# A higher cost in the list scheduler for the sums of a triple over the columns of a bank

## Chip, cores and metric

The kernel runs on one core of one Trainium2 chip. The metric is the device time of one execution in microseconds (us); lower is better. All times below are in us unless they are marked ns.

## What is computed

A gated linear attention (heads of 48 channels, 4 batches, 8 heads, 768 positions) is followed by a bilinear feed-forward block on its output (3072 tokens, model width 384, inner width 1536). Everything is float32.

```python
f = 1.0 / (1.0 + np.exp(-f_logit))
for t in range(S):
    state = f[:, :, t, :, None] * state + np.einsum('bhd,bhe->bhde', k[:, :, t], v[:, :, t])
    y[:, :, t] = np.einsum('bhd,bhde->bhe', q[:, :, t], state)
x = y.transpose(0, 2, 1, 3).reshape(B * S, H * D)
out = ((x @ w_a) * (x @ w_b)) @ w_out
```

## The kernel before

**Blocks and units.** The tokens are worked in 8 blocks of 384 (half a sequence of one batch). The attention of one block is done in two units of four heads each. A unit has a *front* and a *core*. The front (`front_parts`) is on ScalarE two sigmoids (L326 writes `inv`, L323 writes f), on GpSimd one affine step (L329), and on VectorE two running products of f (L333, 384 columns each), a small comparison (L336), a reciprocal (L341), six running products of `inv` (L346, 128 columns each), and the products k·inv and q·F (L350, into `k_in` and `q_in`). The core is on TensorE scores (L403), transposes of k (L428), gains of the state (L452), and the two parts of the output, `within` (L501) and `across` (L527), with VectorE's mask (L416, tile `at`), ScalarE's copy of the turned k (L437, tile `kT`), VectorE's states (L479, L481, L490), ScalarE's copies of the output (L546) and SyncE's transfers into `xT` (L566). Unit s's scores follow `within` of the unit before it in one step (`within_and_scores`), so L501 and L403 stand together.

**Feed-forward.** Blocks 0 and 1 multiply with both weights plainly (`up`, L610). From block 2 on, `up_triples` (L732) uses a scheme of 15 products of half blocks in place of 18, four times for each block (j = 0 to 3). Each of the 15 beats puts 2 matmuls of 192 columns (four records in the trace) into one PSUM bank of four (`ps_f`). A bank is then emptied, either by ScalarE's copy (L1319) or by VectorE's sum of the bank's 2x192 columns onto a partial result, `add` inside `up_triples` (L724, tiles `sums` or `groups`). There are five such sums in each round j (r2, r3, u4, t2, u5), 120 in all. Larger L724 instructions sum or multiply 768 or 1152 columns of copied parts in SBUF. `down` (L834) multiplies with the output weights and has small sums of its own (L863, L866, L869). Combinations of the inputs are formed in `combine_x` (L716 on VectorE, L645 on ScalarE).

**What sets the order.** Every engine works its queue in the order in which the program emits instructions, and a planner in `by_quotients` chooses this order while the program is built. The list `main` holds the feed-forward steps in a fixed order; each is a tuple made by `on_pe` or `on`: the engine, a cost in ns, a due beat, and the function to call. Beside it stand six lines of optional steps (`for_out`, `for_x`, `core`, `fore`, `loads`, `for_ba`), each in order within itself. Ahead of each main step, `fill` takes as many optional steps as fit: a TensorE step when its inputs are planned to be ready, another engine's step when it can start within one beat (653 ns) and when `delays` finds that it would not push a main step of that engine past its due beat. The planner keeps its own clock: `now` for TensorE and `free_at` for each other engine, moved on by each step's cost. A cost therefore changes no instruction; it changes which optional steps the planner finds room for at which place.

```python
def delays(engine, start, load):
    with_it, without, copied = start + load, free_at[engine], max(free_at[ACT], last_copy)
...
        with_it, without = (max(x, ready) + cost for x in (with_it, without))
        if with_it + MARGIN > max(starts.get(due, 1 << 30), without + MARGIN):
            return True
```

Of the kernel before, what the change touches and what calls it, by code (L numbers as in the profile page):

```python
# [153 lines left out]
def by_quotients(ctx, tc, q, k, f_logit, v, moe_w_a, moe_w_b, moe_w_out, out, ident, weights, bad, ps_f):  # L154
# [149 lines left out]
    PE, DVE, ACT, POOL, SP = range(5)  # L304
# [273 lines left out]
    def products(blk):  # L578

        first = (NTG, 0)[blk] if blk < 2 else blk % 2  # L580
        return groups[:, first:first + NTG].rearrange("p g (k t) -> p g k t", k=NFT)
# [7 lines left out]
    def on_pe(load, do, *args):  # L589
        beats[0] += 1  # L590
        return PE, load, 0, do, *args

    def on(engine, load, due, do, *args, copied=False):
        return engine + COPIED * copied, load, beats[0] + due if due else 1 << 30, do, *args
# [131 lines left out]
    def up_triples(blk):  # L726

        to, tail = products(blk), None

        def emit(ps, name, j, start):  # L730
            for g in range(2):
                nc.tensor.matmul(  # L732
                    ps[:, g],
                    lhsT=sums_of_w[name][:, g, 128 * j:128 * j + 128],
                    rhs=sums_of_x[blk][name],
                    start=start and g == 0,
                    stop=True,
                    skip_group_check=True,
                )

        def times(ps, name, j, start=False):
            return on_pe(BEAT, emit, ps, name, j, start)

        def copy(due, x, ps):
            return on(ACT, 400, due, nc.scalar.copy, x, ps)

        def finish(j, c, out, v):
            yield times(v, "v6", j)
            yield copy(5, out[1, 0], v)
            a, b = (  # L750
                c[:, g].rearrange("p k i t -> p k (i t)").rearrange("p k (g t) -> p g k t", g=NTG) for g in range(2)
            )
            yield on(DVE, 1280, 0, add_steps, to.rearrange("p g (k j) t -> p j g k t", k=NI)[:, j], a, b, ALU.mult, copied=True)

        for j in range(NJ3):
            v, u, r, t = (ps_f[i][:, 0:BLK].rearrange("p (g t) -> p g t", g=2) for i in free)
            free[:] = [free[i] for i in ((2, 1, 3, 0) if j < NJ3 - 1 else (2, 3, 1, 0))]
            c = (sums, last[:, 0:2 * NI * BLK])[j % 2].rearrange("p (g k i t) -> p g k i t", g=2, k=NI, i=2)
            out = {(k, i): c[:, :, k, i] for k in range(NI) for i in range(2)}
            if j % 2:  # L760
                at = thirds.index(down_first[0])
                pairs = [thirds[(at + n) % 3] for n in (1, 2)]
            else:
                pairs = [last[:, PIECE * n:PIECE * n + PIECE] for n in range(2)]
            first, second = (x.rearrange("p (g n t) -> p g n t", g=2, n=2) for x in pairs)

            def add(due, k, i, ps, copied=False):
                return on(DVE, 470, due, add_steps, out[k, i], ps, out[k, i], copied=copied)

            yield times(v, "v1", j, True)  # L770
            yield copy(3, out[2, 0], v)
            if tail:
                yield from finish(*tail)
            yield times(u, "u1", j, True)
            yield copy(3, out[1, 1], u)
            yield times(r, "r2", j, True)
            yield add(6, 1, 1, r, True)
            yield times(v, "v2", j)
            yield copy(3, out[2, 1], v)
            yield times(u, "u2", j)  # L780
            yield copy(3, first[:, :, 1], u)
            yield times(t, "t1", j, True)
            yield copy(6, out[0, 0], t)
            yield times(v, "v3", j)
            yield copy(3, first[:, :, 0], v)
            yield on(DVE, 870, 0, add_steps, c[:, :, 1:3, 1], c[:, :, 1:3, 1], first, copied=True)
            yield times(u, "u3", j)
            yield copy(3, out[0, 1], u)
            yield times(r, "r3", j, True)
            yield add(6, 2, 1, r)  # L790
            yield times(v, "v4", j)
            yield copy(3, second[:, :, 1], v)
            yield times(u, "u4", j)
            yield add(3, 0, 0, u)
            yield times(t, "t2", j)
            yield add(5, 0, 1, t)
            yield times(v, "v5", j)
            yield copy(2 if j == NJ3 - 1 else 3, second[:, :, 0], v)
            yield times(u, "u5", j)
            yield add(3, 2, 0, u)  # L800
            yield on(DVE, 870, 0, add_steps, c[:, :, 0], c[:, :, 0], second, copied=True)
            tail = j, c, out, v
        yield from finish(*tail)
# [868 lines left out]
```

## Time and profile before

| what | value |
|---|---|
| median of 3 runs | 594.78 (593.83 to 594.9) |
| the profiled execution | 595.13 |
| its span in the profile | 593.4 |
| TensorE matmul busy | 571.1 |
| VectorE busy | 412.1 |
| ScalarE busy | 256.8 |
| L724 sums of 2x192 columns from PSUM, both tile names | 60 at 552 ns and 60 at 549 ns |
| L732, the triples' matmuls of 192 columns | 1440 records, 326 to 331 ns each |
| L834, the output's matmuls of 192 columns | 1008 records, 326 to 329 ns each |

A row of the profile gives an instruction's place in the code (L724 is line 724), its engine, what it writes and reads by the program's tile names, how often it ran, and its mean duration. PE is TensorE's matmuls, PEld its weight loads, DVE is VectorE, ACT is ScalarE, POOL is GpSimd, SP is SyncE. Matmuls overlap: two records of 192 columns start 163 ns apart though each lasts twice that. An arrow with an engine's name behind idle time tells which instruction ended it.

### The profile page before, as it was taken

How to read it: one execution, taken by the hardware profiler on the slowest of the kernel's cores; microseconds unless marked ns; L12 is line 12 of the kernel's file. 1: busy time of each engine (PE TensorE's matmuls, PEld its weight loads, DVE VectorE, ACT ScalarE, POOL GpSimd, SP SyncE). 2: the span in 40 equal slices, each digit the busy share in tenths (PEclk: the TensorE clock that was granted, in tenths of full speed). 3: DMA queues.
4: the chain of work that ended last, by engine and by line, in shares of the span. 5: the costliest groups of instructions: out<-in, count | busy, mean ns of one | idle time of the engine just before them, and what ended most of it. 6: DMA issues, size and time to landing. Idle time of an engine off the chain costs nothing.

```text
span 593.4 us, 13932 instructions
## 1 busy us (share of the span) xinstructions
PE 571.1 (96%) x5802; PEld 511.8 (86%) x5802; DVE 412.1 (69%) x786; ACT 256.8 (43%) x487; POOL 89.0 (15%) x72
## 2 busy tenths in 40 slices
PE   2899999999999999999999999999999999999996
PEld 1655655557999999999999999999999999999996
DVE  6999445599978678958895678847785165835751
ACT  5577848653122464235521444326431335135300
POOL 7365637454000000000000000000000000000000
PEclk9999999999999999999999999999999999999999
DMA  8696689089552440044004410041001100000001
GB/s 216 183 253 207 221 263 272 0 150 186 114 144 70 115 93 11 15 119 97 2 1 127 109 22 2 2 106 42 3 1 48 48 2 0 2 28 1 0 29 32
DMA packets 33560, 49.42 MB, mean 83 GB/s; under 512 B 3984, under 2 KB 25264, under 8 KB 33488
## 3 DMA queue, kind: packets, MB, share of 16 engines
q1 hardware_dynamic: 30000, 42.19, 25.8%
q0 software_dynamic: 3056, 5.92, 5.9%
q8 instruction: 47, 0.77, 0.6%
q10 hardware_dynamic: 432, 0.34, 0.2%
q14 instruction: 25, 0.20, 0.1%
HBM read 33.23 MB, written 4.72 MB: 64 GB/s over the span
## 4 chain that ended last, share of the span: by engine, by line
PE 84%; DVE 11%; issue 2%; ACT 1%; DMA 1%; SPq 0%; DVEq 0%; ACTq 0%
PE ps_f L732 35%; PE ps_f L834 28%; PE ps_f L610 13%; PE ps_y L501 2%; DVE inv L346 2%; PE ps_y L527 2%; PE ps_x L403 2%; PE ps_x L452 1%; DVE sums L724 1%; PE ps_x L428 1%; DVE groups L724 1%; DVE w_ba L83 1%; DVE q_in L350 1%; DVE f_in L333 1%; DVE spare L346 1%
## 5 line engine op out<-in xcount | busy, mean ns | idle before, releaser
L610 PE MATMUL ps_f<-xT,w_ba 128*128 128x384 f32 x288 | 95.6, 489 | 1.5 <-DMA xT<-y 1.4
L1319 ACT COPY sums<-ps_f 128x384 f32<-128x384 f32 x120 | 57.5, 480 | 75.8 <-PE ps_f L732 62.2
L610 PEld LDWEIGHTS ps_f<-xT,w_ba 128*128 128x128 f32 x288 | 53.9, 190 | 38.2 <-issue 2.2
L1319 ACT COPY groups<-ps_f 128x384 f32<-128x384 f32 x120 | 57.8, 482 | 64.3 <-PE ps_f L732 41.9
L732 PE MATMUL ps_f<-xT,w_ba 128*128 128x192 f32 x384 | 78.3, 326 | 0.0
L732 PEld LDWEIGHTS ps_f<-xT,w_ba 128*128 128x128 f32 x384 | 64.8, 190 | 0.1
L73 POOL TENSOR_SCALAR sums<-sums 128x768 f32<-128x768 f32 (+1 forms) x20 | 52.2, 2612 | 35.8 <-ACT sums L71 35.6
L732 PE MATMUL ps_f<-groups,w_ba 128*128 128x192 f32 x288 | 55.3, 328 | 0.0
L732 PE MATMUL ps_f<-x_sums,raw 128*128 128x192 f32 x288 | 53.8, 331 | 1.1 <-DVE groups L724 0.9
L329 POOL TENSOR_SCALAR inv<-inv 128x768 f32<-128x768 f32 x14 | 12.9, 923 | 265.9 <-ACT inv L326 265.8
L834 PE MATMUL ps_f<-w_out,sums 128*128 128x192 f32 x288 | 52.1, 329 | 0.3 <-DVE groups L632 0.3
L834 PE MATMUL ps_f<-w_out,groups 128*128 128x192 f32 x288 | 51.7, 328 | 0.0
L732 PEld LDWEIGHTS ps_f<-x_sums,raw 128*128 128x128 f32 x288 | 47.0, 190 | 4.1 <-DVE groups L724 2.1
L834 PE MATMUL ps_f<-spare,sums 128*128 128x192 f32 x288 | 49.0, 326 | 0.0
L732 PEld LDWEIGHTS ps_f<-groups,w_ba 128*128 128x128 f32 x288 | 47.9, 190 | 0.5 <-ACT groups L1319 0.2
L834 PEld LDWEIGHTS ps_f<-w_out,sums 128*128 128x128 f32 x288 | 47.1, 190 | 1.0 <-DVE groups L632 0.6
L834 PEld LDWEIGHTS ps_f<-w_out,groups 128*128 128x128 f32 x288 | 47.1, 190 | 0.7
L834 PEld LDWEIGHTS ps_f<-spare,sums 128*128 128x128 f32 x288 | 47.1, 190 | 0.1
L724 DVE TENSOR_TENSOR sums<-sums,groups 128x768 f32<-128x768 f32 x36 | 34.7, 964 | 13.4 <-ACT groups L1319 13.0
L724 DVE TENSOR_TENSOR sums<-ps_f,sums 128x384 f32<-128x384 f32 x60 | 32.9, 552 | 15.9 <-PE ps_f L732 14.0
L732 PE MATMUL ps_f<-x_sums,w_ba 128*128 128x192 f32 x192 | 39.4, 328 | 0.5 <-DVE sums L724 0.5
L732 PE MATMUL ps_f<-xT,raw 128*128 128x192 f32 x192 | 39.6, 329 | 0.0
(142 smaller groups left out, 851.0 us busy)
## 6 DMA issues: line engine op xcount, KB each, us to landing
raw<-w_ba POOLq DMA_DIRECT2D x11, 512.0 KB, 8.5
k_in<-in_k_dram SPq DMA_DIRECT2D x32, 144.0 KB, 4.4
q_in<-in_q_dram SPq DMA_DIRECT2D x32, 144.0 KB, 4.3
v_in<-in_v_dram SPq DMA_DIRECT2D x16, 288.0 KB, 5.7
raw<-in_moe_w_out_dram SPq DMA_DIRECT2D x6, 768.0 KB, 5.6
out_dram<-o SPq DMA_DIRECT2D x22, 192.0 KB, 1.9
f_in<-in_f_logit_dram SPq DMA_DIRECT2D x28, 144.0 KB, 3.1
xT<-y SPq DMA_DIRECT2D x45, 72.0 KB, 2.1
```

What stands on the lines that cost most here:

```text
L73: nc.gpsimd.tensor_scalar(h, h, HI_MIN, HI_MAX, ALU.max, ALU.min)
L83: nc.vector.tensor_tensor(dst[:, rows], hu[:, rows], bit[:, rows], ALU.add)
L329: nc.gpsimd.tensor_scalar(inv, inv, EXP_K, 1.0, ALU.mult, ALU.add)
L346: nc.vector.tensor_tensor_scan(inv[:, w], inv[:, w], none[:, 0:C], first, ALU.mult, ALU.add)
L403: nc.tensor.matmul(ps[h][SUB * p:SUB * p + SUB, o:o + SUB], lhsT=kf[r, tokens(n, c, p)], rhs=qf[r, tokens(n, c, p)], start=True, stop=True,)
L501: nc.tensor.matmul(ps[p][e:e + D, o:o + SUB], lhsT=t["v"][r, n, c, h * D:h * D + D], rhs=at[r, h, o:o + SUB], start=o == 0, stop=True, ski ...
L527: nc.tensor.matmul(ps[p][e:e + D, o:o + SUB], lhsT=st[j][r, n], rhs=qf[r, tokens(n, c, p)], start=False, stop=True, skip_group_check=True,)
L610: nc.tensor.matmul(ps[nm][:, 0:BLK], lhsT=w[:, kt, ft * 128:ft * 128 + 128], rhs=xT[blk][:, kt], start=kt == 0, stop=kt == NKT - 1,)
L724: nc.vector.tensor_tensor(to, x, y, op)
L732: nc.tensor.matmul(ps[:, g], lhsT=sums_of_w[name][:, g, 128 * j:128 * j + 128], rhs=sums_of_x[blk][name], start=start and g == 0, stop=Tru ...
L834: nc.tensor.matmul(to, lhsT=x[:, i // 2, i % 2], rhs=w[:, NI * (i % 2) + i // 2], start=start and i == 0, stop=i == HFT - 1, skip_group_ch ...
L1319: do(*args)
```

## The change

One number changes: the cost, in ns, under which the planner enters each of the 120 sums of `add` in `up_triples`.

```diff
             def add(due, k, i, ps, copied=False):
-                return on(DVE, 470, due, add_steps, out[k, i], ps, out[k, i], copied=copied)
+                return on(DVE, 550, due, add_steps, out[k, i], ps, out[k, i], copied=copied)
```

The tuple's other entries, the due beats among them, stay. The costs of the larger sums (870 and 1280), of ScalarE's copies (400) and of the optional steps stay as well.

## Prediction

> **What bounds the kernel now.** I read the page's busy table first, then the weight loads' waits after 125 us, then stretches of time, then the instructions in order of time.
>
> ```profile
> PE 571.1 (96%) x5802; PEld 511.8 (86%) x5802; DVE 412.1 (69%) x786; ACT 256.8 (43%) x487; POOL 89.0 (15%) x72
> ```
>
> TensorE is the bound. The change can give only what TensorE loses inside the planned part; matmul time itself stays. Who holds it up there:
>
> ```profile
> PEld ps_f L732 <- DVE groups L724: 2.1, 4, 1.2
> PEld ps_f L732 <- DVE sums L724: 1.4, 3, 0.8
> PEld ps_f L732 <- ACT sums L1319: 1.0, 4, 0.3
> PEld ps_f L732 <- ACT groups L1319: 0.6, 2, 0.4
> ```
>
> The columns are total us, times, longest. About 5 us lie before triples (L732), and most of it behind VectorE's sums (L724), which free a PSUM bank. By stretch (PE, PEld, DVE, ACT, POOL busy):
>
> ```profile
> 225.00:229.00 4.00, 3.54 (x22) 3.24 (x21) 3.74 (x7) 0.61 (x2) 0.00 (x0) 1.00 0.02 6
> 277.00:303.00 26.00, 25.14 (x295) 23.74 (x297) 23.31 (x39) 12.58 (x26) 0.83 (x1) 1.00 0.01 2
> 303.00:347.00 44.00, 44.00 (x571) 42.79 (x561) 28.93 (x63) 12.98 (x29) 0.94 (x2) 1.00 0.34 87
> 347.00:357.00 10.00, 9.75 (x58) 9.26 (x58) 8.85 (x17) 5.52 (x12) 0.72 (x1) 1.00 0.00 1
> ```
>
> TensorE has holes where VectorE is 9/10 busy; at 303 to 347, VectorE is idle a third of the time and TensorE has none. The two largest holes, in order of time (start, us):
>
> ```profile
> 225.39 2.11 PE L732 MATMUL ps_f<-x_sums,raw 128*128 128x192 f32 x12
> 225.53 0.53 DVE L724 TENSOR_TENSOR sums<-ps_f,sums 128x384 f32<-128x384 f32 x1
> ...
> 226.48 0.96 DVE L350 TENSOR_TENSOR k_in<-k_in,inv 128x768 f32<-128x768 f32 x1
> 227.36 0.55 DVE L724 TENSOR_TENSOR sums<-ps_f,sums 128x384 f32<-128x384 f32 x1
> ...
> 227.96 0.92 PE L732 MATMUL ps_f<-x_sums,w_ba 128*128 128x192 f32 x4 [0.46 <-DVE sums L724]
> ```
>
> ```profile
> 297.01 0.96 DVE L350 TENSOR_TENSOR k_in<-k_in,inv 128x768 f32<-128x768 f32 x1
> ...
> 299.62 1.48 DVE L724 TENSOR_TENSOR groups<-ps_f,groups 128x384 f32<-128x384 f32 x3
> ...
> 300.69 1.27 PEld L732 LDWEIGHTS ps_f<-x_sums,raw 128*128 128x128 f32 x8 [1.15 <-DVE groups L724]
> 300.69 1.57 PE L732 MATMUL ps_f<-x_sums,raw 128*128 128x192 f32 x8 [0.86 <-DVE groups L724]
> 301.02 0.95 DVE L350 TENSOR_TENSOR q_in<-q_in,f_in 128x768 f32<-128x768 f32 x1
> ```
>
> Both times a k_in product that nobody needs yet stands before a sum for which TensorE waits. In both the next beat (four matmul records, 0.65) comes late.
>
> **What the Trainium skill says.** (1) "Perfetto Trace Analysis", section DVE / Act Engine Instruction: the profiled interval ends with the write's acknowledgement, and the next instruction may start before that. The trace agrees: a sum lasts 0.55 alone, yet three in a row start 299.62, 300.09, 300.56 and the next instruction at 301.02, so 0.47 each. The old 470 was the spacing, the new 550 is the duration; on a full queue the planner now counts 0.08 too much per sum. (2) "PSUM — Partial Sum Buffer", section Engine vs sequencer instructions: VectorE's and ScalarE's queues are strictly first in, first out, so work put ahead of a sum delays it in full. That is what the two holes show.
>
> **The change part by part.** No instruction is added or removed: 120 sums (60 + 60 in the page's groups) are entered 80 ns dearer, and the planner puts optional steps elsewhere. I compared the built orders of both. Nothing differs before 225 us. GpSimd's order is the same; on SyncE one output store passes one xT copy near 466, whose block is used after 522, so it costs nothing. ScalarE's two sigmoids (L326, L323) go behind one or two copies at 232 and 284, and other copies trade places near 248 and 263; none then frees a bank later than its next beat. The count of switches between matmul kinds stays, so their 0.1 to 0.25 each cancel.
>
> For each hole I relaid VectorE's queue by hand in the new order, with spacings from neighbouring rows of the trace: sum 0.46, product or sum of 768 columns 0.87, of 1152 1.28, scan of 384 0.86, scan of 128 0.31 to 0.39 (0.50 before one that needs its result), mask 0.88. A beat is ready for VectorE 0.85 after it starts (366.00 to 366.85); a sum lets TensorE go 0.60 after its start (300.09 to 300.69), a copy 0.52 to 0.55. A restart costs another 0.10.
>
> 1. *228.* k_in goes from 226.48 to behind the sum of 231.03. Queue: sum 225.14, sum 225.14+0.45, two scans 0.89, sum at 226.48 instead of 227.36. It frees the bank at 227.08; TensorE arrives at 226.69+0.65 = 227.34. The hole of 0.62 and its restart go, and the three copies behind it (228.86 on, with two more restarts) come 0.9 earlier. The bank of the beat that was at 230.16 is then free at 229.29, just when TensorE gets there. Gain 0.85 (0.75 to 0.95). k_in and q_in now end at 232.4, against the scores' need at 233.3.
> 2. *251.* One scan and a reciprocal (0.40) go to the front; the sum L863 comes earlier; a restart of 0.10 goes.
> 3. *277.5.* Two scans fall behind the sum of 276.91, which starts at 276.24; hole 0.15 and restart gone: 0.25.
> 4. *293.* The second 768-column sum comes 0.5 earlier, because a scan of f falls behind it; three copies stop being late: 0.3. Here L501 and L403 (scores) move three beats back, so the mask waits for them till about 288.2 and VectorE is idle from 286.6. Behind it the sum for the bank wanted at 291.4 frees it at 291.0: it fits by 0.38.
> 5. *300.7.* k_in and q_in leave for 310 and later, where VectorE has room. The 768-column sum can start once its copy is done at 296.0; then 0.87+0.87+0.46+0.31 leads to the sum at 298.5, bank free at 299.1. TensorE, 0.55 earlier by steps 3 and 4, wants it at 299.2. Hole 1.02 and restart 0.10 go; about 0.2 comes back, because in the last quarter of a triple the copy of one beat and the matmul two beats on are too close anyway (the same 0.08 to 0.14 plus a restart stands at 376.5, 437.4, 507.5, 560.3). Gain 0.87. Their scores at 316.8-1.7 find q_in done 2 us before.
> 6. *356.* A scan falls behind two sums; first of them at 355.13, bank at 355.72, wanted 355.86: hole 0.28 and restart gone, 0.38. The hole of 0.40 at 347.2 stays: ScalarE's sigmoid makes it, and its order there is unchanged.
> 7. *414.7.* The same: 0.19.
> 8. *428.* New: L428 goes one beat (0.65) later, the kT copy and the copy behind it with it; that one frees its bank at 428.09, wanted 428.00: a hole of 0.09 and a restart, minus 0.19 (0 to 0.3).
>
> Sum: 0.85+0.10+0.25+0.30+0.87+0.38+0.19-0.19 = 2.75, with 0.1 each way from rounding per step; TensorE ends the chain from 303 to the end, so it arrives in full. The profiled execution took 595.13 (span 593.4 and 1.7 around it), which would become 592.4; the runs' median is 0.35 below that execution: 594.78-2.75 = 592.0.
>
> **The rivals.** *A, likeliest:* as summed, 592.0, own range 591.4 to 592.6. *B, the hole at 300.7 stays in part:* step 5 has a margin of 0.1 only. For: VectorE's queue there has nine steps in a row without slack. Against: it starts from a copy, not from older lateness. It gives back up to 0.9: 592.9. *C, the holes move on:* VectorE's work is the same, and the next sum is late instead; only 228 and 356 (with k_in off their queue or ample room behind) help, and the copies at 428 and 293 take 0.4: 594.78-0.85-0.38+0.4 = 593.95. Against it: VectorE idles a third of 303 to 347. *D, slower:* the mask wait of step 4. A strictly ordered queue stands idle 1.6 behind scores that were put later, with two sums, two scans and the sum that three copies wait for behind it; the same at 422 to 424 (1.2). It decides once the sum behind the mask is more than 0.38 later than laid out; then both idle times show as TensorE holes and steps 2 to 5 and 7 are lost: +1.6+1.2+0.2-0.85-0.38 = 1.8, 596.6. Against: the mask followed its scores by 0.95 to 1.15 in every case before. That nothing happens at all is excluded, as the built order differs.
>
> **How the numbers follow.** A 0.60, B 0.22, C 0.10, D 0.08. Two tenths of a per cent (1.2 us) is about what a measurement of this kernel can tell from no change. A and B are faster, 0.82; C is within, 0.10; D is slower, 0.08. A and B hold 0.82, so the range runs from the floor (all that these holes and restarts hold is some 4 us, less the 0.4 of the sigmoid: 591.2, and 0.2 for rounding: 591.0) to the top of B with its rounding: 593.6.
>
> **What would show it.** Step 1: no TensorE wait near 228, a k_in product after the sum at 231. Steps 3 to 5: TensorE busy 26 of 26 in 277 to 303, but for 0.2 at its end; VectorE idle about 1.6 ahead of the mask. Step 6: no wait near 355, one of 0.3 near 345 still there. Step 8: a short wait on a copy near 426. I am wrong if the TensorE wait for L724 after 225 stays above 1.5 us in total, or if L403 waits for q_in.

## The result, and the profile after

| | before | after |
|---|---|---|
| median, run beside each other on one chip | 595.25 (592.52 to 599.22, 17 runs) | 592.67 (590.37 to 594.15, 17 runs) |
| ratio after / before, 95% interval | | 0.9949 (0.9936 to 0.9962) |
| the profiled execution | 595.13 | 593.61 |
| its span | 593.4 | 591.8 |

The changed kernel is faster by 2.6 us by the medians, and by 2.3 to 3.8 by the ratio's interval. 592.67 lies 0.67 above the predicted 592.0 and inside the range; 0.47 of the 0.67 is the starting point, since the kernel before has 595.25 here and had 594.78 in the three runs from which the prediction counted.

The same views, in the same order, of the changed kernel. First the busy table:

```profile
PE 571.0 (96%) x5802; PEld 512.0 (87%) x5802; DVE 412.3 (70%) x786; ACT 257.5 (44%) x487; POOL 89.0 (15%) x72
```

Work is the same on every engine to within 0.7 us; 1.6 us of span are gone, so they were idle time. Then the waits of the weight loads after 125 us (total, times, longest):

```profile
PEld ps_f L732 <- ACT sums L1319: 1.2, 5, 0.3
PEld ps_f L732 <- DVE sums L724: 0.8, 3, 0.3
PEld ps_f L732 <- ACT groups L1319: 0.6, 2, 0.4
```

The wait for `DVE groups L724` (2.1) is gone, and the one for `DVE sums L724` has gone from 1.4 to 0.8: VectorE's sums hold TensorE 0.8 in place of 3.5. Waits for ScalarE went up by 0.2. By stretch (PE, PEld, DVE, ACT, POOL busy):

```profile
225.00:229.00 4.00, 4.00 (x27) 3.99 (x26) 3.75 (x9) 0.75 (x3) 0.00 (x0) 1.00 0.02 4
277.00:303.00 26.00, 26.00 (x327) 25.14 (x326) 23.67 (x41) 12.84 (x26) 0.83 (x1) 1.00 0.01 2
303.00:347.00 44.00, 43.86 (x532) 42.64 (x531) 30.23 (x63) 13.91 (x30) 1.67 (x2) 1.00 0.34 86
347.00:357.00 10.00, 10.00 (x62) 9.79 (x62) 8.76 (x17) 4.74 (x11) 0.00 (x0) 1.00 0.01 2
```

TensorE is busy 4.00 of 4, 26.00 of 26 and 10.00 of 10. The 0.14 that is now missing in 303 to 347 is the hole of the sigmoid, which has come 1.5 us earlier and so crossed the edge of the stretch. VectorE is busy within 0.4 of before in each stretch, but for 1.3 more in 303 to 347, where the k_in and q_in of unit 12 have gone. The two places of the largest holes, in order of time, 228 first:

```profile
227.35 0.54 DVE L724 TENSOR_TENSOR sums<-ps_f,sums 128x384 f32<-128x384 f32 x1
...
228.33 0.81 PE L732 MATMUL ps_f<-x_sums,w_ba 128*128 128x192 f32 x4
...
231.48 0.95 DVE L350 TENSOR_TENSOR k_in<-k_in,inv 128x768 f32<-128x768 f32 x1
```

```profile
298.50 1.00 DVE L724 TENSOR_TENSOR groups<-ps_f,groups 128x384 f32<-128x384 f32 x2
...
299.09 1.65 PE L732 MATMUL ps_f<-x_sums,raw 128*128 128x192 f32 x8
```

The matmul rows carry no "idle before": the sum starts 0.98 ahead of its matmul at 228, and 0.59 ahead at 299. A sum needs 0.60, so the second place has no slack left. The k_in product of unit 9 is at 231.48, that of unit 12 at 310.21.

**Where the time came from.** The feed-forward matmuls (L610, L732, L834) have the same order in both kernels, so record i of one trace answers to record i of the other. The table gives by how much they start *earlier* than in the kernel before (below: the *lead*), set to zero at 225 us, where the orders begin to differ. The places are times of the trace before; each column is the same count for a kernel of the experiments below, from one profiled execution of each.

| up to | after | e1 | e2 | e3 | e4 | e5 | e6 | e7 | e8 | e9 |
|---|---|---|---|---|---|---|---|---|---|---|
| 229 | 0.72 | 0.72 | 0 | 0.72 | 0 | 0.72 | 0 | 0.72 | 0.54 | 0 |
| 240 | 0.97 | 0.97 | 0 | 0.96 | 0 | 0.97 | 0.19 | 0.36 | 0.54 | 0 |
| 252.5 | 1.09 | 1.09 | -0.01 | 0.99 | -0.01 | 1.09 | 0.30 | 0.48 | 0.54 | 0.01 |
| 279 | 1.34 | 1.33 | 0.24 | 1.22 | 0 | 1.34 | 0.54 | 0.74 | 0.54 | 0.01 |
| 292 | 1.34 | 1.02 | 0.10 | 0.86 | -0.01 | 0.64 | 0.23 | 0.74 | 0.54 | 0.01 |
| 296 | 1.57 | 1.00 | 0.22 | 0.84 | -0.01 | 0.68 | 0.21 | 0.96 | 0.54 | 0.01 |
| 302 | 2.51 | 1.15 | 0.92 | 0.99 | 0.93 | 1.62 | 0.36 | 1.90 | 1.09 | 0.01 |
| 357.5 | 2.78 | 1.11 | 0.92 | 0.97 | 0.46 | 1.93 | 1.01 | 2.10 | 1.03 | 0.32 |
| 370 | 2.61 | 1.11 | 0.92 | 0.97 | -0.43 | 1.76 | 1.02 | 2.10 | 1.03 | 0.15 |
| 417 | 2.85 | 1.11 | 0.92 | 0.97 | -0.43 | 2.00 | 1.06 | 2.33 | 1.03 | 0.38 |
| the end | 2.71 | 1.08 | 0.92 | 0.92 | -0.43 | 1.86 | 0.92 | 2.33 | 1.03 | 0.23 |

This table decides more than the times do. The profiled execution of after is only 1.52 faster than that of before, mainly because its matmuls were already 0.93 later at 81 us, in a part where the two programs are the same (the last section comes back to it).

### The profile page after: what moved, and what is told of

It is laid out like the page before. It is cut to its first block, busy times and chain, and to the rows that moved or that the text cites. A ratio compares the mean times of both kernels' runs of the same rounds, so it can differ in the third digit from the quotient of the medians.

```text
span 591.8 us, 13934 instructions
## 1 busy us (share of the span) xinstructions
PE 571.0 (96%) x5802; PEld 512.0 (87%) x5802; DVE 412.3 (70%) x786; ACT 257.5 (44%) x487; POOL 89.0 (15%) x72
## 4 chain that ended last, share of the span: by engine, by line
PE 89%; DVE 7%; issue 2%; ACT 1%; DMA 1%; SPq 0%; DVEq 0%; ACTq 0%
PE ps_f L732 40%; PE ps_f L834 28%; PE ps_f L610 13%; PE ps_y L501 2%; PE ps_y L527 2%; PE ps_x L403 2%; PE ps_x L452 1%; PE ps_x L428 1%; DVE inv L346 1%; DVE w_ba L83 1%; DVE q_in L350 1%; DVE spare L346 1%; DVE groups L333 1%; DVE st L481 1%; DMA f_in<-in_f_logit_dram 1%
## 5 line engine op out<-in xcount | busy, mean ns | idle before, releaser
L610 PE MATMUL ps_f<-xT,w_ba 128*128 128x384 f32 x288 | 95.5, 489 | 0.1
L610 PEld LDWEIGHTS ps_f<-xT,w_ba 128*128 128x128 f32 x288 | 53.9, 190 | 36.8 <-issue 0.7
L732 PE MATMUL ps_f<-xT,w_ba 128*128 128x192 f32 x384 | 78.4, 327 | 0.0
L732 PEld LDWEIGHTS ps_f<-xT,w_ba 128*128 128x128 f32 x384 | 64.8, 190 | 0.2
L732 PE MATMUL ps_f<-groups,w_ba 128*128 128x192 f32 x288 | 55.2, 327 | 0.0
L732 PE MATMUL ps_f<-x_sums,raw 128*128 128x192 f32 x288 | 54.2, 331 | 0.2
L834 PE MATMUL ps_f<-w_out,sums 128*128 128x192 f32 x288 | 52.1, 329 | 0.3 <-DVE groups L632 0.3
L834 PE MATMUL ps_f<-w_out,groups 128*128 128x192 f32 x288 | 51.7, 328 | 0.0
L732 PEld LDWEIGHTS ps_f<-x_sums,raw 128*128 128x128 f32 x288 | 46.9, 190 | 2.8 <-ACT sums L1319 1.2
L834 PE MATMUL ps_f<-spare,sums 128*128 128x192 f32 x288 | 49.0, 326 | 0.0
L732 PEld LDWEIGHTS ps_f<-groups,w_ba 128*128 128x128 f32 x288 | 48.0, 190 | 0.2
L834 PEld LDWEIGHTS ps_f<-w_out,sums 128*128 128x128 f32 x288 | 47.1, 190 | 1.0 <-DVE groups L632 0.6
L834 PEld LDWEIGHTS ps_f<-w_out,groups 128*128 128x128 f32 x288 | 47.1, 190 | 0.7
L834 PEld LDWEIGHTS ps_f<-spare,sums 128*128 128x128 f32 x288 | 47.1, 190 | 0.1
L724 DVE TENSOR_TENSOR sums<-sums,groups 128x768 f32<-128x768 f32 x36 | 34.7, 965 | 13.8 <-ACT groups L1319 13.3
L724 DVE TENSOR_TENSOR sums<-ps_f,sums 128x384 f32<-128x384 f32 x60 | 32.7, 553 | 16.1 <-PE ps_f L732 14.5
L732 PE MATMUL ps_f<-xT,raw 128*128 128x192 f32 x192 | 39.2, 327 | 0.0
L732 PE MATMUL ps_f<-x_sums,w_ba 128*128 128x192 f32 x192 | 39.2, 327 | 0.0
```

Source lines behind the costliest of these rows:

```text
L610: nc.tensor.matmul(ps[nm][:, 0:BLK], lhsT=w[:, kt, ft * 128:ft * 128 + 128], rhs=xT[blk][:, kt], start=kt == 0, stop=kt == NKT - 1,)
L724: nc.vector.tensor_tensor(to, x, y, op)
L732: nc.tensor.matmul(ps[:, g], lhsT=sums_of_w[name][:, g, 128 * j:128 * j + 128], rhs=sums_of_x[blk][name], start=start and g == 0, stop=Tru ...
L834: nc.tensor.matmul(to, lhsT=x[:, i // 2, i % 2], rhs=w[:, NI * (i % 2) + i // 2], start=start and i == 0, stop=i == HFT - 1, skip_group_ch ...
```

## The experiments

Theory: TensorE loses time where the release of one bank stands in a strictly ordered queue behind a long optional step, and the gain is the sum of such places. Rivals: the gain of one place is lost at the next (rival C); the mask wait eats it (rival D); it is the accuracy of the number as such that pays. A "hole" below is how much later a matmul record starts than such records otherwise follow one another (0.163); a "restart" is a second delay of 0.10, two records further on. Each time stands beside the kernel before on the same chip: 595.55 for e1 to e4, 595.45 for e5 to e8, 595.67 for e9 to e12.

### e1 and e2: the change in one block alone

```diff
-                return on(DVE, 470, due, add_steps, out[k, i], ps, out[k, i], copied=copied)
+                return on(DVE, 550 if blk == 2 else 470, due, add_steps, out[k, i], ps, out[k, i], copied=copied)
```

> The cost of 550 for block 2's sums alone, 470 in the other blocks. My theory (what counts is which optional VectorE step stands directly before a sum that frees a bank): block 2's order becomes the one of the changed kernel, so the hole at 228 us and its restarts go (0.95 us) and a restart near 251 (0.1). In block 3 the built order has the k_in product moved from ahead of two 768-column steps to a place directly before the sum for which TensorE waited at 300.7; the work ahead of that sum stays the same, so a hole of about 1 us should remain there. Total gain in the planned part 1.0 to 1.4 us (about 593.6 where before is 594.8). Rival (any work moved out of block 2 makes the whole later plan lighter): the hole near 300 shrinks too, gain 2 us or more.

Measured: 594.57, ratio 0.9984 (0.9967 to 1.0002). The interval takes in no change; the trace shows a lead of 1.08 at the end. All of it is there by 279 (1.33), and a hole of 0.87 stays at 300, where k_in stands ahead of the sum.

> The cost of 550 for block 3's sums alone. Theory: nothing changes before 275 us, so the hole of 0.62 near 228 stays; the hole of 0.15 near 277.5 goes (0.25 with its restart), and near 300.7 the k_in product and one running product fall behind the sum, which comes 0.9 us earlier, so 0.8 to 1.0 us of the hole goes. Gain 1.0 to 1.5 us. Rival (the gain at 300 needed the lead won in block 2): the hole at 300.7 stays above 0.7, gain 0.3 us.

Measured (`blk == 3`): 594.63, ratio 0.9986 (0.9973 to 0.9999), a lead of 0.92, slightly under the 1.0 expected. The hole of 0.62 at 228 stays, the one at 300.7 shrinks from 1.02 to 0.32.

What follows: the blocks give their gains each at its own places, but they don't add up. e1, e2 and e9 sum to 2.23, the whole change has 2.71. The 0.24 at 277.5 is in both e1 and e2, and 0.67 is in neither: between 279 and 302 the changed kernel gains 1.17, the three runs together 0.50. In e1, TensorE comes to 288 1.3 us earlier, and there three short front steps stand directly ahead of a sum, as in the kernel before, and a scan of f directly ahead of these; two restarts of 0.10 appear with a short wait, and 0.31 of the lead is lost by 292. In the changed kernel that order changes too, and nothing is lost.

### e3 and e4: one product held back, costs as before

```diff
+                *steps, k_step, q_step = [(e, load, 0, *do) for part in front_parts(s) for e, load, *do in part]
+                fore.extend(steps, needs=loaded), fore.extend((k_step,), past={9: 248}.get(s, 0))
+                ready = fore.extend((q_step,))
```

The planner may not place the k_in product of unit 9, nor what stands behind it in its line, before the step of `main` with the number 248; e4 has `{12: 458}`, for unit 12. All costs are those of the kernel before.

> The sums keep the cost of 470; one k_in product, the one at 226.5 us, is held back by hand until the main step before which the changed kernel issues it. Theory: it was this product alone that stood before the sum; hole near 228 gone, 0.9 us gained there, although no cost was changed; other places keep their holes but for small shifts, total gain 0.7 to 1.3 us. Rival (the planner's better timing of all sums counts, not one step): the hole moves to the next sum, gain under 0.3 us.

Measured: 594.06, ratio 0.9981 (0.997 to 0.9993), a lead of 0.96 at 240 as in the changed kernel (0.97), and 0.92 at the end. Step 1 comes whole from holding that product back, with every sum still counted at 470. Behind 240 the leads follow those of e1 to within 0.16, with a hole of 0.88 at 300.

> As the run before, with the k_in product at 297.0 us (and the q_in product behind it) held until the place where the changed kernel has them, at 311 us. Theory: the sum before TensorE's wait at 300.7 starts 0.88 us earlier, so the hole of 1.02 us falls to 0.15; about 0.2 comes back from the copy and matmul that are too close at the end of the triple; gain 0.7 to 0.9 us, and the hole near 228 stays at 0.62. Rival as before: gain under 0.3 us.

Measured: 595.22, ratio 1.0001 (0.9987 to 1.0015). The expectation missed in its total. The hole at 300.7 went as foreseen (lead 0.93), and then more than the lead was lost, down to -0.43 by 370. The first place of the loss, in order of time:

```profile
310.53 0.95 DVE L350 TENSOR_TENSOR q_in<-q_in,f_in 128x768 f32<-128x768 f32 x1
311.39 0.35 DVE L863 TENSOR_TENSOR u<-ps_f,u 128x192 f32<-128x192 f32 x1
311.80 0.92 PE L834 MATMUL ps_f<-spare,groups 128*128 128x192 f32 x4 [0.34 <-DVE u L863]
```

k_in and q_in now stand together ahead of a sum of `down`, a hole of 0.50; further ones of 0.15 at 346.5 and 0.54 at 357.1 (a q_in ahead of a sum again) follow. This is rival C. With 550 the k_in went to almost the same time (310.21), but q_in was put behind the sum L863 (311.08) and starts at 311.81; no hole followed.

### e5: the mask twice

```diff
-        nc.vector.tensor_tensor(to, x, tri.broadcast_to((128, 2, 2 * NC, SUB)), ALU.mult)
+        for _ in range(1 + (u == 11)):
+            nc.vector.tensor_tensor(to, x, tri.broadcast_to((128, 2, 2 * NC, SUB)), ALU.mult)
```

> The changed kernel with the causal mask of unit 11 multiplied twice in place of once (the product of a 0/1 mask, so the second pass leaves the values as they are). It tests the price of rival D and the margin of step 4. Theory (the queue of VectorE is in order, and what counts is how late the sum behind a long product is against TensorE's need): at 291 us the sum for bank 3 ends 0.9 us later, against a margin of about 0.4, so TensorE gets a new hole there of 0.4 to 0.6 us and restarts 0.1 later; nothing later gives it back; the kernel is 0.5 to 0.7 slower than the changed one, so 2.0 to 2.2 us faster than the kernel before. Rival (the mask lies beside work that has room for it): the same time as the changed kernel within 0.2, no hole at 291.

Measured: 593.4, ratio 0.9967 (0.9956 to 0.9979). The end has a lead of 1.86, so 0.85 less than the changed kernel; 0.5 to 0.7 had been expected. In order of time (lines are one further down in this kernel):

```profile
287.78 1.95 DVE L417 TENSOR_TENSOR at<-ps_x,causal 128x768 f32<-128x768 f32 x2 [1.48 <-PE ps_x L403]
...
289.78 0.58 PEld L429 LDWEIGHTS ps_x<-ident,k_in 112*128 112x128 f32 x6 [0.19 <-DVE at L417]
...
290.97 0.53 DVE L725 TENSOR_TENSOR sums<-ps_f,sums 128x384 f32<-128x384 f32 x1
...
291.56 0.92 PE L733 MATMUL ps_f<-x_sums,w_ba 128*128 128x192 f32 x4 [0.32 <-DVE sums L725]
```

The hole of 0.48 behind the sum and its restart (0.10) are the theory's. Two terms had been left out. The transposes write the tile that the mask reads, so they wait for the second mask as well (holes of 0.06 and 0.05). And the later lateness keeps the two holes of step 4 at 293 and 294 (0.07 and 0.10), which the changed kernel has lost. So rival D's mechanism is real, and the margin of step 4 fits: the sum starts 3.19 behind the start of the mask in place of 2.20, so 0.99 later; less the 0.11 that TensorE had lost at the transposes and the margin of 0.38, this leaves 0.50, and the hole is 0.48. In the changed kernel this margin held:

```profile
288.10 0.96 DVE L416 TENSOR_TENSOR at<-ps_x,causal 128x768 f32<-128x768 f32 x1 [1.48 <-PE ps_x L403]
...
290.30 0.53 DVE L724 TENSOR_TENSOR sums<-ps_f,sums 128x384 f32<-128x384 f32 x1
...
291.29 0.81 PE L732 MATMUL ps_f<-x_sums,w_ba 128*128 128x192 f32 x4
```

VectorE stands idle 1.48 ahead of the mask; the sum still starts 0.99 before its matmul, and needs 0.60.

### e6, e7 and e10: other numbers

The edit is the same line with 510, 630 and 800.

> The kernel before with the cost 510 in place of 470, half the way to 550. Rival (the nearer the planner's number is to the duration on the chip, the better): half the gain of the changed kernel, 1.3 us. Theory (only the order counts that results, and in it which bank's release lands behind a long product): in this order the product of k and the reciprocals of unit 9 stands directly ahead of the third sum at 228, as before, so the hole of 0.62 there stays and its 0.97 is not gained; at 300.7 the product stands between the first and the second sum of the group, so part or all of the 0.9 there is gained; the orders of steps 2 to 4 are those of the changed kernel, 0.3 to 0.6; total 0.9 to 1.6 us. Both theories overlap in the total, so the verdict is the places: the hole at 228 stays whole for the theory.

Measured: 594.18, ratio 0.9975 (0.9964 to 0.9986), a lead of 0.92. The places: the hole of 0.62 at 228 stays whole, as expected. The one at 300.7 is still 0.87, where part or all had been expected to go; instead the sigmoid's hole at 345 and the one at 356 went (0.65 between 302 and 357.5). Step 4, which had been expected as in the changed kernel, brought a loss of 0.33 by 296. The times alone would fit "half way gives half".

> The kernel before with the cost 630, which is as far above the 0.55 us on the chip as 470 is below it. Rival (accuracy of the number is what pays): it loses as much as 470 does, so about the time of the kernel before, or at most half of the gain. Theory (the order counts): in this order the product of unit 9 stands behind the third sum as in the changed kernel, so 0.97 at 228 is gained; the product of unit 12 has moved behind the sum that waited at 300.7 as well, 0.6 to 0.9; total 1.5 to 2.8 us faster than before, so an overestimate costs nothing or little here.

Measured: 593.12, ratio 0.9963 (0.9948 to 0.9978), a lead of 2.33. The overestimate by 80 ns keeps most of the gain where the underestimate by 80 had none of it. It has a hole of its own, on ScalarE's queue:

```profile
238.65 0.72 ACT L437 COPY kT<-ps_x 128x672 f32<-128x672 f32 x1 [3.35 <-PE ps_x L428]
...
239.26 0.48 ACT L1319 COPY sums<-ps_f 128x384 f32<-128x384 f32 x1
...
239.80 0.92 PE L732 MATMUL ps_f<-x_sums,raw 128*128 128x192 f32 x4 [0.52 <-ACT sums L1319]
```

The transposes were put one beat later, so ScalarE, idle for 3.35, has the copy of the turned k just when it should free a bank: a hole of 0.69.

> The kernel before with the cost 800. Rival (a cost that is high enough keeps the front products out of the way): at least the gain of the changed kernel, 2.5 us or more. Theory (only the order counts): with this cost the product of k of unit 9 stands directly ahead of the third sum at 228 again, as in the kernel before, so the hole of 0.62 and its 0.97 us stay; the mask of unit 11 stands ahead of the sum that it delays as in the kernel before, too; at 300.7 the place isn't clear, between no gain and 0.9. Total 0 to 1.4 us faster than before, so 1.2 us or more behind the changed kernel.

Measured: 594.22, ratio 0.9982 (0.9969 to 0.9995), a lead of 0.79 at the end. What the expectation says of the order is wrong: in this kernel the trace has the product of unit 9 at 231.62, behind all three sums, and no hole above 0.2 behind a sum or copy from 228 to 360. The total falls in the expected span for another reason, and is no support for it. The gain was made and then lost at 361.0 (0.32), 407.4 (0.67) and 423.7 (0.57). The last of these has the old form, once more with a k_in:

```profile
422.22 0.96 DVE L350 TENSOR_TENSOR k_in<-k_in,inv 128x768 f32<-128x768 f32 x1
...
423.09 1.02 DVE L724 TENSOR_TENSOR sums<-ps_f,sums 128x384 f32<-128x384 f32 x2
...
423.70 1.08 PE L732 MATMUL ps_f<-x_sums,raw 128*128 128x192 f32 x5 [0.41 <-DVE sums L724]
```

At 407.4 it is a sigmoid (L326, from 405.59) ahead of two copies. So the higher cost of 800 doesn't keep optional steps away from the sums; it puts them elsewhere. By the traces the leads are 0 (470), 0.92 (510), 2.71 (550), 2.33 (630), 0.79 (800). This series doesn't fit "the nearer to 550 the better": 510 is 40 away and has 0.92, 630 is 80 away and has 2.33.

### e8: half of the product

```diff
-            nc.vector.tensor_tensor(halves(t[nm]), halves(t[nm]), by, ALU.mult)
+            half = slice(0, BLK if nm == "k" and u in (9, 12) else 2 * BLK)
+            nc.vector.tensor_tensor(halves(t[nm])[:, half], halves(t[nm])[:, half], by[:, half], ALU.mult)
```

> The kernel before, in its own order, with the product of k and the reciprocals done for one of the two head pairs only in units 9 and 12 (it leaves out the other half of that product, so the output of those units differs). It tells whether the length of that one instruction, 0.88 us, is what made the two holes. Theory: with some 0.45 us less ahead of the sums, the hole of 0.62 at 228 shrinks to about 0.2 and the one of 1.0 at 300.7 to about 0.55, so 0.8 to 1.0 us faster than the kernel before. Rival (the sums themselves are late, through the matmuls that they read or through DVE's own pipeline): the holes stay as long, and the time is within 0.2.

Measured: 594.25, ratio 0.9977 (0.9964 to 0.9989), a lead of 1.03. In order of time:

```profile
226.68 0.53 DVE L351 TENSOR_TENSOR k_in<-k_in,inv 128x384 f32<-128x384 f32 x1
227.13 0.55 DVE L725 TENSOR_TENSOR sums<-ps_f,sums 128x384 f32<-128x384 f32 x1
...
227.73 0.62 PEld L733 LDWEIGHTS ps_f<-x_sums,w_ba 128*128 128x128 f32 x4 [0.21 <-DVE sums L725]
```

```profile
298.85 1.48 DVE L725 TENSOR_TENSOR groups<-ps_f,groups 128x384 f32<-128x384 f32 x3
...
299.92 1.41 PE L733 MATMUL ps_f<-x_sums,raw 128*128 128x192 f32 x7 [0.32 <-DVE groups L725]
```

At the first place the sum follows the product after 0.45 in place of 0.88, and the product follows its scan after 0.39 in place of 0.50: 0.54 earlier in all. The hole at 228 goes from 0.62 to 0.08, the one at 300.7 from 1.02 to 0.48, and the leads gained there are 0.54 and 0.55. The expectation had 0.2 for the first, since it left out the 0.11. With the order unchanged, TensorE starts earlier by just what was taken off ahead of the sum, so the time that this one product takes in the queue was the cause.

### e9: blocks 4 and later

The edit is that of e1 with `blk >= 4`.

> The kernel before with 550 for the groups of blocks 4 and later only, 470 for those ahead. It tells how much of the small steps 6 to 8, and of the loss at 366, comes from these blocks by themselves. Theory: the holes at 228 and 300.7 stay whole; only the places after 350 change, and TensorE ends 0.1 to 0.3 us earlier than before, mostly from 414.7; a time within 0.5 of the kernel before. Rival: steps 6 to 8 come from the earlier groups, whose shift the planner carries on, and nothing changes here (0.0).

Measured: 594.61, ratio 0.9983 (0.9969 to 0.9997); the lead is 0.23, all of it behind 350. It repeats steps 6 to 8 of the changed kernel to 0.02: +0.31 at 356, -0.17 by 370, +0.23 at 415, -0.15 at 428. They come from these blocks alone. The medians are 1.06 apart, more than the trace can account for.

### e11 and e12: more costs made true

```diff
-            yield PE, 760, 0, turn, s
+            yield PE, 600, 0, turn, s
```

> The changed kernel with one more planner cost set to the duration on the chip: TensorE's turn of k (six transposes) is counted with 600 in place of 760; the trace shows 0.58. It is a try for a version that beats both. If an accurate number pays by itself: 0.2 to 0.6 us faster than the changed kernel. Theory (each change of a cost redraws the places of the front products, and only holes count): TensorE's order changes from unit 3 on, new holes of 0.3 to 0.7 as likely as old ones gone; between 0.5 faster and 1.5 slower than the changed kernel, and still 1 us or more faster than the kernel before.

> As the run before it, and the planner's cost of the step with the gains and the part across chunks set from 1550 to 1350 as well. The same two readings: 0.3 to 0.8 us faster than the changed kernel if accuracy pays by itself; between 0.5 faster and 1.5 slower if the order is what counts, with the holes at other places than in the run with 600 alone.

Measured: e11 593.71, ratio 0.9971 (0.996 to 0.9982); e12, which has 1350 for 1550 as well, 593.22, ratio 0.996 (0.9945 to 0.9974). Here the orders differ before 225 too; counted from 81 us the leads are 1.44 and 2.20, against 2.66 for the changed kernel. So e11 is 1.2 slower than it and e12 0.5, by the traces; the intervals of the ratios overlap with its own. The largest new holes stand at 202.4 (0.70) and 251.9 (0.64) in e11, at 235.0 (0.51) in e12. A number nearer to the chip did not pay by itself. No version beat the changed kernel.

## Why the prediction was right

| step | predicted | measured |
|---|---|---|
| 1, at 228 to 240 | 0.85 (0.75 to 0.95) | 0.97 |
| 2, at 251 | 0.10 | 0.12 |
| 3, at 277.5 | 0.25 | 0.25 |
| 4, at 293 | 0.30 | 0.23 |
| 5, at 300.7 | 0.87 | 0.94 |
| 6, at 356 | 0.38 | 0.30, then -0.17 at 366 |
| 7, at 414.7 | 0.19 | 0.24 |
| 8, at 428 | -0.19 (0 to -0.3) | -0.14 |
| sum | 2.75 | 2.71 |

The rows leave out 0.03 lost at 350. Seven of eight terms are within 0.12. That the sums agree to 0.04 is partly luck: step 1 misses by 0.12 upward and step 6, with its loss, by 0.25 downward. Step 1 lies above its own range; the hole at 228 and the three restarts that go with it are 0.92 already.

**Steps 1 and 5**, two thirds of the sum, rest on single instructions: e3 and e4 each take one of them away and gain that place, e8 shortens both and gains in measure. They also show in numbers what the Trainium skill says in "PSUM — Partial Sum Buffer", section Engine vs sequencer instructions, that VectorE's and ScalarE's queues are first in, first out: 0.54 less ahead of the sum in e8 became 0.54 on TensorE.

**Step 4** had its risk named with the right size: the margin predicted as 0.38 was 0.99 less 0.60, so 0.39, and e5 shows what lies beyond it. Rival D is excluded for the changed kernel by the sum at 290.30. At the second place that D names, VectorE is idle 0.91 ahead of the mask at 422.50, and no new hole follows but the small one of step 8. That the hole at 291 opens past about 0.4 fits e5; no smaller delay was tried.

**Step 6 is mis-sized.** Its gain at 356 was 0.30, but 0.17 went back at 366, which the prediction doesn't list. There, behind k_in and q_in, a 768-column sum starts at 362.13 and three column sums follow:

```profile
362.13 0.95 DVE L724 TENSOR_TENSOR sums<-sums,groups 128x768 f32<-128x768 f32 x1
...
363.18 1.49 DVE L724 TENSOR_TENSOR sums<-ps_f,sums 128x384 f32<-128x384 f32 x3
...
364.26 1.92 PEld L732 LDWEIGHTS ps_f<-x_sums,raw 128*128 128x128 f32 x12 [0.20 <-DVE sums L724]
```

The bank of the second of them (363.66) is free at 364.26, where TensorE wants it at 364.20, and the restart makes the rest. Ahead of k_in stand two running products here, from 359.50, and one in the kernel before (361.29): a front step that made room at 356 is in the way at 366. The prediction followed the queue up to the hole that closes and not down to the next place where it runs without slack. e9 shows the same loss with nothing else changed.

**Rivals.** B (the hole at 300.7 stays in part) is not what happened, but it was close: TensorE took the bank at 299.09, without delay, but just when the sum of 298.50 let it go, so the margin of 0.1 was used up. In e2, with block 3 alone, 0.32 stays. C is not what happened either, but e4 shows it is no idle fear: the same product moved by hand to nearly the same time gave everything back. The two kernels differ there in the place of q_in, behind the sum at 311.08 in the changed one; why the planner finds it with 550, and whether this alone kept C away, was not followed. **The reason for the gain is therefore the resulting order, not the true number.** That is shown for the single holes (e3, e4, e8, e10) and for another cost (e11). On a full queue the sums follow one another after 0.47, so as a spacing the old 470 was as true as the new number is as a duration. It is not shown that 550 is the best value: 510, 630 and 800 give less, and no number between was tried.

By the signs named ahead: VectorE's sums hold TensorE 0.8 in total, under the 1.5; L403 has one wait for q_in of 0.7, the same as in the kernel before, near 130 and outside the plan's changes; the hole of the sigmoid stays with 0.30 at 345.74; a wait of 0.17 on a copy stands at 426.37.

## What to carry to other kernels

In a kernel whose bound engine is fed through strictly ordered queues, look at each of its holes for what stands directly ahead of the late instruction, and ask whether anybody needs it yet; the time that this one instruction takes in the queue (0.88 here), less the slack that the late instruction had, plus the restarts, is the price of the hole. When a step is moved, by hand or by a planner's cost, follow its new queue past the gain, to the next place without slack, before counting it. A planner's cost is a knob on the order: judge a value by the holes in the trace of the order that it gives, not by how well it agrees with a duration.

## What the runs showed that was not expected

- **The scatter comes ahead of the part that was changed.** The matmuls at 81 us stand between 1.40 us earlier (e3) and 3.17 later (e6) than in the profile before, though up to there these programs run the same instructions. From 81 to 225 the offset moves by at most 0.14 in those whose order doesn't differ there. Differences of 0.2 to 1 us can be read from matched instructions after that point, not from medians of some twenty runs.
- **A restart has a price of its own.** In all kernels here, between 220 us and the end, every hole above 0.11 between two feed-forward matmuls is followed by another 0.10 ahead of the second pair of its beat: at 228 and 300.7 before, at 291.83 in e5, at 407.69 and 423.96 in e10.
- **A chain of copies passes a hole on.** The hole of 0.62 at 228 cost 0.97: 0.92 of this is the hole itself and three restarts (0.10 at 228.23, 229.66 and 230.43); the last two are of matmuls whose banks ScalarE's copies free late, since these wait for the same run of VectorE's queue. In e8, where queue and TensorE both come 0.54 earlier, all three restarts stay.
